# Loading order, wk's transpose and a rewritten order table in a fused attention and FFN kernel

## The chip, the core and the metric

The kernel runs on one core of a Trainium2 chip. Times are device microseconds (us) of one execution; the comparison is between medians of runs of the kernel before and the kernel after. PE is the tensor engine (PEld its weight loads), DVE the vector engine, ACT the scalar engine, POOL GpSimd, SP the engine that here only issues DMAs.

## What is computed

For 2048 tokens of width 640, `g * a + (1 - g) * b`: a gate of its own for each token, a linear attention `a` of 32 heads of 20, and a gated FFN `b` of width 1728.

```python
qkv = x @ wqkv                                        # q, k, v, each [32 heads, 2048, 20]
pq, pk = q @ w_phi, k @ w_phi                         # for each head
phi = lambda p: concat(softmax(p), softmax(-p))       # 40 features for each head
kv, z = phi(pk).T @ v, phi(pk).sum(over tokens)
o = (phi(pq) @ kv) / (phi(pq) @ z + 1e-6)
a = o @ wo
b = (silu(x @ w_gate) * (x @ w_up)) @ w_down
g = sigmoid((x * gate_w).sum(-1))
```

## The kernel before, in words

The tokens are cut into 16 tiles of 128 (`NT`), and for the FFN and the output into four blocks of 512. Everything is bf16 with sums in PSUM. All instructions are written out once, and `_Tracker` puts the semaphore waits in. What the program does is a list of items, `ORDER`, in which each item is a letter, a tile or block, and sometimes a part. An engine's instructions run in the order in which the items stand in this list, so the list is the schedule of all five engines. The items:

- `H` warming matmuls on ones (`NWARM` = 4 each); `G` gate_w's column, put beside wv; `X t` five PE transposes of an x tile (`xpose`).
- `V t` v of a tile and the gate's sum; `U` the first V tiles, their five chunks of wv interleaved, so that the work starts when the first chunk lands.
- `W m` five PE transposes of a row block of wk into `wT` (`wxpose`); `Y` w_phi laid out as blocks `wbd`; `M m` and `R m` premultiply wk and wq with w_phi (`premult`), so that k's and q's projections give pk and pq at once.
- `K t` projects a k tile, takes exp(p) and exp(-p) on ACT into `ekr`, sums (DVE), reciprocals (DVE), and the product with them on POOL. `E t` adds phi(k).T v into PSUM banks 6 and 7, which the item `I` takes out of the ring of pairs of banks and `N` (`kv_finish`) puts back. `Z` broadcasts z by matmul into `zb`.
- `Q t` projects a q tile and takes both exponentials into `eq` (three buffers); `A` sums them (`qz`, DVE); `B` is the DVE product `ez` = eq * zb; `C` gives the denominators on DVE, then the scaled phi(q) `ph` on POOL and its transposing DMA to `phiT` on SP's queue.
- `F b.k` 128 columns of w_gate and w_up for a block: ten matmuls of 512 columns, tanh and a copy on ACT, a product on DVE that reads PSUM, a product on POOL into `hT`. `O b.part` is phi(q) times kv, `D b.u` one output tile: 19 pairs of matmuls with `wd`, `wog`, an ACT scaling by the gate, the store.
- `L` issues the loads of all FFN weights and of wo; `T` copies the last 64 columns of the two FFN weights side by side; `J` gives the gates.

Loads stand ahead of the list. SP's queue has x tile 0, three chunks of wv, then transposing DMAs of x tiles 2 and 3, five plain loads of wk, and transposing DMAs of x, wq and x. ACT's has gate_w, x tile 1, two chunks of wv and w_phi. `ring` gives out four pairs of PSUM banks in turn (three while the kv sums stand), and an item that gets a pair waits until its last user has been read out. `slab` is one stretch of SBUF with different tiles in different stages.

The lines that the prediction names are helpers': L284 is every matmul, L296 PE's transposes, L302 ACT, L308 copies, L312 products of two tensors (`tt`), L316 and L323 DVE, L337 and L338 transposing and plain DMAs.

Of the kernel before, what the change touches and what calls it, by code (L numbers as in the profile page):

```python
# [14 lines left out]
NCH = 11  # L15
NPE = 2
NV = 6
# [11 lines left out]


ORDER = """
H2 H0 H3 H1 L H5 H4 G X0 X1 U V2 W0 W1 Y V3 W2 W3 I W4 M2 M1 M0 M4 M3 K0 K1 K2 V4 K3 V5 R0 E0 V6
E1 K4 V7 K5 R1 E2 K6 E3 V8 K7 V9 E4 V10 E5 K8 K9 E6 V11 E7 R3 K10 K11 R2 E8 F0.0 E9 V12 K12 K13
F0.1 E10 V13 K14 E11 R4 F0.2 K15 V14 Q0 A0 V15 E12 F0.3 E13 E14 E15 N F1.0 Q1 A1 Z B0 F0.4 J Q2
C0 F1.1 B1 F1.2 C1 F1.3 F0.5 A2 Q3 F0.6 F0.7 A3 B2 F0.8 F1.4 F0.9 B3 Q4 F0.10 T C2 F1.5 F1.6 C3
F1.7 F0.11 A4 F1.8 Q5 Q6 F0.12 F0.13 F1.9 F1.10 A5 O0.0 B4 O0.1 O0.2 F1.11 B5 F1.12 C4 A6 Q7 B6
D0.0 C5 A7 Q8 C6 D0.1 D0.2 B7 Q9 C7 A8 F1.13 D0.3 Q10 A9 B8 F2.0 C8 A10 O1.0 O1.1 B9 O1.2 F2.1
F2.2 C9 Q11 B10 C10 D1.0 F2.3 Q12 A11 B11 D1.1 D1.2 Q13 F2.4 F2.5 A12 A13 F2.6 F2.7 F2.8 C11 F2.9
D1.3 B12 C12 F2.10 F3.0 F2.11 B13 Q14 A14 F3.1 Q15 A15 F3.2 F2.12 B14 F3.3 O2.0 C13 F2.13 F3.4
F3.5 B15 F3.6 O2.1 O2.2 F3.7 F3.8 C14 D2.0 F3.9 D2.1 C15 F3.10 F3.11 F3.12 O3.0 O3.1 O3.2 F3.13  # L40
D2.2 D2.3 D3.0 D3.1 D3.2 D3.3
"""
# [145 lines left out]
def _build(nc, A_x, A_wqkv, A_w_phi, A_wo, B_x, B_w_gate, B_w_up, B_w_down, gate_w, out):  # L188
# [30 lines left out]
    omg = sb("omg", [P, NT], F32)  # L219
    ksum = sb("ksum", [P, 2, 64], F32)  # L220
    krec = sb("krec", [P, 2, 66], F32)
    v1r = sb("v1r", [P, NV, 33 * 21], BF16)
# [9 lines left out]

    hbase = nc.lookup_mloc(hT).addr
    ekr = nc.alloc_sbuf_tensor_at("ekr", [P, 4, FK], BF16, offset=hbase + 14 * 512 * 2)
    tr.reg(ekr, "sbuf", hbase + 14 * 512 * 2)

# [14 lines left out]
    oT = at("oT", [P, 2, 5, 512], BF16, 2 * 4 * NCH * P * 2)  # L251
    xs = at("xs", [P, 6, D], BF16, 0)
    wkn = at("wkn", [P, 5, D], BF16, 7680)
    wTq = at("wTq", [P, 5, 5, P], BF16, 14080)
    wT = at("wT", [P, 5, 5, P], BF16, 20480)
    wbd = at("wbd", [P, 5, 160], BF16, 26880)
    wph = at("wph", [P, 5, DH], BF16, 28480)
    bmask = at("bmask", [P, 5, 8], BF16, 28736)
    gwr = at("gwr", [P, P], BF16, 28864)

# [67 lines left out]
    def memset(e, a, v):  # L328
        eo = tr.eng[e]
        return run(e, lambda: eo.memset(a, v), [], [a])  # L330
# [16 lines left out]


    x2 = A_x[0]
    out2 = out[0]  # L350

    def load_x(t, e="sp"):
        if t < NPE:
            dma(e, xs[:, t, :], x2[t * P:(t + 1) * P, :])
        else:
            dma("sp", xT[:, t, :, :], x2[t * P:(t + 1) * P, :], transpose=True)

    def load_rows(e, dst, c, c0):
        dma(e, dst, A_wqkv[c * P:(c + 1) * P, c0:c0 + D])

    dma("act", gwr[0:5, :], bass.AP(gate_w.tensor, gate_w.offset, [[P, 5], [1, P]]))
    load_x(0)
    load_x(1, "act")
    for c in range(5):
        load_rows("act" if c % 2 else "sp", wvg[:, c, 0:D], c, 2 * D)
    load_x(2)
    dma("act", wph[:, :, :], A_w_phi.rearrange("h e f -> (h e) f").rearrange("(c p) f -> p c f", p=P))
    load_x(3)
    for c in range(5):
        load_rows("sp", wkn[:, c, :], c, D)  # L370
    for t in range(4, 7):
        load_x(t)
    for m in range(5):
        dma("sp", wTq[:, m, :, :], A_wqkv[m * P:(m + 1) * P, 0:D], transpose=True)
    for t in range(7, NT):
        load_x(t)
    memset("pool", ident[:, :], 0.0)
# [6 lines left out]
    for c in range(5):  # L384
        b0 = P * c - DH * H0[c]
        select(bmask[:, c, :], [[-DH, 8]], ALU.is_ge, 0.0, b0, 1)
        select(bmask[:, c, :], [[DH, 8]], ALU.is_gt, 0.0, DH - b0, -1)
    v1v = v1r[:, :, :].rearrange("p b (h d) -> p b h d", d=DH + 1)
    memset("dve", ones[:, :], 1.0)
    memset("dve", v1v[:, :, H, :], 0.0)  # L390
    memset("dve", v1v[:, :, :, DH:DH + 1], 1.0)
    memset("dve", ekr[:, :, 1280:FK], 0.0)
# [9 lines left out]

    def load_ffn_weights():
        for c0, c1 in ((0, 512), (512, 1152), (1152, F_FFN)):
            dma("sp", wg[:, :, c0:c1], B_w_gate[:, c0:c1].rearrange("(c p) j -> p c j", p=P))
            dma("sp", wu[:, :, c0:c1], B_w_up[:, c0:c1].rearrange("(c p) j -> p c j", p=P))
        dma("sp", wd[:, 0:13, :], B_w_down[0:13 * P, :].rearrange("(c p) j -> p c j", p=P))
        dma("sp", wd[0:64, 13, :], B_w_down[13 * P:F_FFN, :])
        wo_a = A_wo[0:600, :].rearrange("(m s r) j -> s r m j", s=2, r=60)
        dma("sp", wog[0:60, :, :], wo_a[0])  # L410
        dma("sp", wog[64:124, :, :], wo_a[1])
        dma("sp", wd[64:104, 13, :], A_wo[600:640, :])
# [35 lines left out]
    def v_out(t, pr):  # L448
        i = halves(pr).rearrange("p b (h d) -> p b h d", d=DH)
        o = v1v[:, t % NV, 0:H, 0:DH].rearrange("p (b h) d -> p b h d", b=2)  # L450
        copy("act", o, i)
        copy("act", svec[:, t:t + 1], bank(2 * pr + 1, 320, 321))
# [5 lines left out]

    def vfirst():

        prs = [next_pair(), next_pair()]
        pairs = [v_pairs(t, prs[t]) for t in range(2)]
        for c in range(5):
            for t in range(2):
                mm(pairs[t][2 * c:2 * c + 2])
        for t in range(2):
            v_out(t, prs[t])

# [17 lines left out]
    def ktile(t):  # L486
        pr = tok_proj(t, 1, t == 0)
        b = t % 4
        s = t % 2
        e = ekr[:, b, 0:1280]  # L490
        head_exps(pr, e)
        reduce(ksum[:, s, :], e.rearrange("p (g d) -> p g d", d=DH))
        recip(krec[:, s, 0:64], ksum[:, s, :])
        ev = e.rearrange("p (g d) -> p g d", d=DH)
        tt("pool", ev, ev, krec[:, s, 0:64].unsqueeze(2).to_broadcast([P, 64, DH]), ALU.mult)

    KV0 = 6

    def kvtile(t):
        b = t % 4  # L500
        pairs = []
        for j in range(NCH):
            bk, jj = (KV0, j) if j < 8 else (KV0 + 1, j - 8)
            o = bank(bk, 63 * jj, 63 * jj + 63)
            pairs.append((o, ekr[:, b, 120 * j:120 * j + P], v1r[:, t % NV, 63 * j:63 * j + 63],
                          t == 0 and jj == 0, t == NT - 1, True))
        mm(pairs)

    def wxpose(m):
        pr = next_pair()  # L510
        o = bankbf(2 * pr, 640)
        transposes([(o[:, c * P:(c + 1) * P], wkn[:, m, c * P:(c + 1) * P]) for c in range(5)])
        copy("dve", wT[:, m, :, :].rearrange("p c k -> p (c k)"), o)

# [72 lines left out]
    def qscale(t):  # L587
# [13 lines left out]
            in1=qd[:, s, :].unsqueeze(2).to_broadcast([P, 32, 2]), op0=ALU.mult, op1=ALU.mult),  # L601
            [qz[:, b, :], qd[:, s, :], g2[:, t:t + 1]], [qc[:, s, 0:64]])
        f = ph[:, b, :].rearrange("p (j c) -> p j c", c=P)[:, :, 0:120]
        tt("pool", f.rearrange("p j (g d) -> p j g d", d=DH),
# [52 lines left out]
    out_evs = []  # L657

    def ditem(bt, u):
        buf = bt % 2  # L660
# [10 lines left out]
        if t < NT - 1:  # L671
# [3 lines left out]
            return  # L675
        mm(half[0])
        actop(o[:, 0:320], bank(2 * pr, 0, 320), ACTF.Copy, omg[:, t:t + 1])
        out_evs.append(dma("sp", out2[t * P:(t + 1) * P, 0:320], o[:, 0:320]))
        mm(half[1])
        actop(o[:, 320:D], bank(2 * pr + 1, 0, 320), ACTF.Copy, omg[:, t:t + 1])  # L680
        out_evs.append(dma("act", out2[t * P:(t + 1) * P, 320:D], o[:, 320:D]))


# [3 lines left out]
    def kv_end():  # L687
        kv_finish()
        ring["n"] = 4

    ops = {
        "H": lambda i: warm(), "X": xpose, "G": gcol, "U": vfirst, "V": vtile, "W": wxpose,
        "M": lambda m: premult(1, m), "R": lambda m: premult(0, m),
        "K": ktile, "E": kvtile, "L": load_ffn_weights, "T": tail_weights, "J": gates,
        "Y": w_blocks, "I": kv_begin, "N": kv_end, "Z": z_broadcast,
        "Q": qtile, "A": qsum, "B": qden, "C": qscale,
        "F": fitem, "O": oitem, "D": ditem,
    }
    for w in ORDER.split():
        ops[w[0]](*[int(a) for a in w[1:].split(".") if a])  # L700
# [4 lines left out]
def bass_gated_mix__linear_kernel_hedgehog__swiglu_ffn__prompt_kernel(  # L705
    nc: bass.Bass,
    A_x: bass.AP,
    A_wqkv: bass.AP,
    A_w_phi: bass.AP,
    A_wo: bass.AP,  # L710
    B_x: bass.AP,
    B_w_gate: bass.AP,
    B_w_up: bass.AP,
    B_w_down: bass.AP,
    gate_w: bass.AP,
    out: bass.AP,
):
    with nc.Block() as block:
        @block.gpsimd
        def _(g):  # L720
            _build(nc, A_x, A_wqkv, A_w_phi, A_wo, B_x, B_w_gate, B_w_up, B_w_down, gate_w, out)

# [27 lines left out]
```

The softmax here doesn't subtract the row's maximum and nothing guards it: scores larger than these inputs give would overflow.

## Time and profile before

| what | value |
|---|---|
| median of 9 runs | 294.62 us (294.2 to 297.71) |
| the profiled execution, its own time | 295.07 us |
| its span, first to last instruction | 293.1 us |
| HBM read and written | 9.45 MB, 2.62 MB |
| transposing DMAs of x, of wq, of ph | 14, 5, 16 |
| mean granted TensorE clock in the record | 1.000 |

The page's busy times tell how full an engine is, not what a change is worth. The chain of waits names who ended last, a timeline gives each group's start, and the distance from one group's start to the next is its cost on that engine, since matmuls overlap and the time shown for one of them is longer than its pace. The clock's record begins only after the first microseconds; there the pace of equal matmuls tells the clock.

### The profile page before, as it was taken

How to read it: one execution, taken by the hardware profiler on the slowest of the kernel's cores; microseconds unless marked ns; L12 is line 12 of the kernel's file. 1: busy time of each engine (PE TensorE's matmuls, PEld its weight loads, DVE VectorE, ACT ScalarE, POOL GpSimd, SP SyncE). 2: the span in 40 equal slices, each digit the busy share in tenths (PEclk: the TensorE clock that was granted, in tenths of full speed). 3: DMA queues.
4: the chain of work that ended last, by engine and by line, in shares of the span. 5: the costliest groups of instructions: out<-in, count | busy, mean ns of one | idle time of the engine just before them, and what ended most of it. 6: DMA issues, size and time to landing. Idle time of an engine off the chain costs nothing.

```text
span 293.1 us, 4885 instructions
## 1 busy us (share of the span) xinstructions
PE 287.7 (98%) x1971; PEld 174.8 (60%) x1971; DVE 168.4 (57%) x248; ACT 148.6 (51%) x252; POOL 157.5 (54%) x118
## 2 busy tenths in 40 slices
PE   8999999999999999999999999999999999999996
PEld 6767776666445545447765567646454466457774
DVE  2566858656898779269973994077657654110000
ACT  1476767674756555682344833352476642472112
POOL 8719769785258758745451565046755844530000
PEclk9999999999999999999999999999999999999999
DMA  8878799520003102200542025100320203300101
GB/s 211 199 113 111 181 360 361 137 56 0 2 4 70 25 2 49 49 2 9 108 111 61 11 42 121 46 0 0 74 49 0 49 2 72 75 0 25 45 22 46
DMA packets 47048, 21.26 MB, mean 73 GB/s; under 512 B 37106, under 2 KB 47026, under 8 KB 47026
## 3 DMA queue, kind: packets, MB, share of 16 engines
q1 hardware_dynamic: 45784, 20.36, 29.4%
q10 hardware_dynamic: 1242, 0.60, 0.7%
q8 instruction: 15, 0.25, 0.4%
q14 instruction: 7, 0.06, 0.1%
HBM read 9.45 MB, written 2.62 MB: 41 GB/s over the span
## 4 chain that ended last, share of the span: by engine, by line
PE 92%; DVE 3%; DMA 2%; ACT 1%; POOL 1%; issue 0%
PE ps L284 91%; DMA phiT<-ph 2%; POOL ph L312 1%; DVE dz L312 1%; PE ps L296 1%; DVE qw L323 0%; DVE hT L316 0%; ACT hT L302 0%; DVE kvsb L312 0%; DVE wqk L308 0%; ACT v1r L302 0%; ACT osb L302 0%; DVE xT L308 0%; DVE wT L308 0%; DVE qd L326 0%
## 5 line engine op out<-in xcount | busy, mean ns | idle before, releaser
L312 POOL TENSOR_TENSOR hT<-hT,us 128x512 bf16<-128x512 bf16 (+1 forms) x56 | 68.4, 1232 | 60.6 <-DVE hT L316 56.7
L316 DVE SCALAR_TENSOR_TENSOR hT<-hT,ps 128x512 bf16<-128x512 bf16 (+1 forms) x56 | 37.8, 680 | 61.3 <-ACT hT L302 54.2
L284 PE MATMUL ps<-xT,wg 128*128 128x512 bf16 x260 | 64.6, 379 | 0.2
L284 PE MATMUL ps<-xT,wu 128*128 128x512 bf16 x260 | 64.6, 379 | 0.0
L284 PE MATMUL ps<-wd,hT 128*128 128x320 bf16 x448 | 63.7, 299 | 0.0
L302 ACT ACTIVATE hT<-ps 128x512 bf16<-128x512 f32 (+2 forms) x60 | 35.8, 596 | 50.8 <-PE ps L284 50.4
L312 POOL TENSOR_TENSOR ph<-eq,qc 128x1320 bf16<-128x1320 bf16 x16 | 39.8, 2488 | 28.3 <-DVE qc L599 28.3
L284 PEld LDWEIGHTS ps<-wd,hT 128*128 128x128 bf16 x448 | 43.9, 98 | 17.8
L284 PE MATMUL ps<-wqk,xT 128*128 128x320 bf16 x320 | 47.8, 299 | 0.0
L312 POOL TENSOR_TENSOR ekr<-ekr,krec 128x1280 bf16<-128x1280 bf16 x16 | 37.4, 2359 | 16.0 <-DVE krec L326 16.0
L284 PEld LDWEIGHTS ps<-xT,wu 128*128 128x128 bf16 x260 | 25.5, 98 | 30.7
L284 PEld LDWEIGHTS ps<-xT,wg 128*128 128x128 bf16 x260 | 24.9, 98 | 28.5 <-ACT us L302 1.1
L302 ACT ACTIVATE osb<-ps,omg 128x640 bf16<-128x640 f32 (+1 forms) x17 | 12.9, 761 | 55.3 <-PE ps L284 55.3
L284 PEld LDWEIGHTS ps<-wqk,xT 128*128 128x128 bf16 x320 | 30.9, 98 | 13.8 <-ACT wqk L302 0.2
L302 ACT ACTIVATE us<-ps 128x512 bf16<-128x512 f32 (+1 forms) x56 | 33.2, 592 | 0.1
L323 DVE TENSOR_REDUCE ksum<-ekr 128x64 f32<-128x1280 bf16 x16 | 23.4, 1464 | 16.9 <-ACT ekr L302 16.9
L302 ACT ACTIVATE eq<-ps 128x640 bf16<-128x640 f32 x32 | 22.4, 703 | 14.6 <-POOL ph L312 9.6
L302 ACT ACTIVATE ekr<-ps 128x640 bf16<-128x640 f32 x32 | 22.1, 703 | 7.1 <-PE ps L284 6.6
L323 DVE TENSOR_REDUCE qz<-eq 128x64 f32<-128x1280 bf16 x16 | 23.6, 1480 | 3.3 <-ACT eq L302 3.3
L284 PE MATMUL ps<-wvg,xT 128*128 128x320 bf16 (+1 forms) x160 | 25.1, 306 | 0.1
L284 PE MATMUL ps<-wog,oT 128*128 128x320 bf16 x160 | 24.5, 299 | 0.0
L323 DVE TENSOR_REDUCE qw<-ez 128x64 f32<-128x1280 bf16 x16 | 23.6, 1478 | 0.1
(71 smaller groups left out, 191.4 us busy)
## 6 DMA issues: line engine op xcount, KB each, us to landing
out_dram<-osb SPq DMA_DIRECT2D x15, 160.0 KB, 1.9
wd<-in_B_w_down_dram SPq DMA_DIRECT2D x1, 2080.0 KB, 17.1
wkn<-in_A_wqkv_dram SPq DMA_DIRECT2D x5, 160.0 KB, 3.2
wg<-in_B_w_gate_dram SPq DMA_DIRECT2D x1, 800.0 KB, 9.0
wu<-in_B_w_up_dram SPq DMA_DIRECT2D x1, 800.0 KB, 10.6
wog<-in_A_wo_dram SPq DMA_DIRECT2D x2, 375.0 KB, 6.8
wg<-in_B_w_gate_dram SPq DMA_DIRECT2D x1, 720.0 KB, 11.5
wu<-in_B_w_up_dram SPq DMA_DIRECT2D x1, 720.0 KB, 11.7
```

The source lines that it names most:

```text
L284: last = pe.matmul(o, lhsT=l, rhs=r, start=st, stop=sp_, skip_group_check=sk)
L296: last = pe.transpose(o, i, ident[0:k, 0:k])
L302: return run("act", lambda: act.activation(o, i, func, scale=scale), rd, [o])
L312: return run(e, lambda: eo.tensor_tensor(o, a, b, op), [a, b], [o])
L316: return run("dve", lambda: dve.scalar_tensor_tensor(out=o, in0=a, scalar=s, in1=b, op0=op0, op1=op1), rd, [o])
L323: return run("dve", lambda: dve.tensor_reduce(o, i, AX.X, ALU.add), [i], [o])
```

## The change

- x tiles 0 to 3 come by plain loads on SP's and ACT's queues and are transposed on PE; the other 12 by transposing DMA. All loads of x, wv, wk and wq stand in a list `LOADS`, with the first 384 columns of the FFN weights ahead of the transposing DMAs.
- wk is loaded by transposing DMA into `wT`; item `W` is gone.
- v of all 16 tiles is kept: six tiles in `v1r`, ten in `v1x`, which lies where `wd` is loaded later. `L` now holds only w_down and wo and stands after the last E.
- `ekr` moves from the place of `hT`'s second buffer to `slab`, so that F items of block 1 may stand before the last E. `ksum` and `krec` get four buffers.
- `K`'s sums and product become items `S` and `P`, `C`'s product and DMA item `c`. `U` becomes one item for a tile and a chunk.
- The last output tile is made in three pieces (320, 224, 96 columns), the last scaled on DVE.
- The program is no longer wrapped in a block of its own.
- The order table is new.

```diff
-NPE = 2
+NPE = 4
...
+LOADS = """
+x0 w0 x1 w1 w2 x2 w3 w4 x3 f0 h k0 k1 t4 k2 k3 k4 t5 t6 t7 t8 t9 t10 t11 t12 t13 t14 t15 q0 q1 q2 q3
+q4 f1 f2
+"""
 ORDER = """
...
+H2 H4 H0 H1 H3 X0 G X1 U0.0 U0.1 U1.0 U0.2 U1.1 X2 U1.2 U0.3 U1.3 U0.4 U2.0 U1.4 U2.1 X3 U2.2 U2.3
+U2.4 V3 Y F0.1 M0 F0.2 M1 M2 F0.0 M3 M4 V4 K0 S0 K1 V7 K2 I P0 V6 S1 P1 K3 S2 E0 K4 S3 V5 P2 P3
+V14 V15 R1 S4 E1 K5 V9 E2 E3 K6 P4 R4 S5 E4 K7 K8 P5 S6 P6 V12 V8 S7 E5 P7 K9 S8 S9 E6 P8 R0 F1.2
+E7 K10 V13 E8 P9 S10 P10 K12 F1.1 R2 S12 P12 V10 E9 K11 K13 E10 S11 V11 P11 J F0.11 T R3 S13 P13
+F0.4 K14 E11 S14 K15 S15 Q1 P15 F1.13 F0.5 F1.8 F0.13 F1.3 E12 P14 F1.11 A1 E13 F0.10 Q2 E14 E15 N
+Q0 F0.12 A0 Z L B0 F1.9 C0 c0 B2 F1.7 F1.12 Q3 A2 C2 c2 B1 F0.8 F0.6 A3 F0.9 C1 c1 Q5 B3 F1.5 C3
+c3 B5 Q4 F0.7 F1.6 F0.3 A5 A4 F1.4 Q6 B4 F1.0 F1.10 C4 C5 c4 A6 O0.2 O0.0 B6 c5 O0.1 C6 Q7 Q8 D0.0
...
+A15 F2.10 c14 F3.6 F3.9 F2.4 C13 F2.6 F2.7 B15 F3.8 F3.12 c13 D2.0 C15 F3.10 D2.1 c15 F3.4 D2.2
+O3.2 O3.1 O3.0 D2.3 D3.2 D3.1 D3.0 D3.3
 """
...
+    v1x = nc.alloc_sbuf_tensor_at("v1x", [P, NT - NV, 33 * 21], BF16, offset=wdbase)
...
+    ekr = at("ekr", [P, 4, FK], BF16, 0)
+    xs = at("xs", [P, NPE, D], BF16, 10752)
...
+    XQ = ["sp", "act", "act", "sp"]
+    WQ = ["sp", "sp", "act", "sp", "act"]
...
+    def load_ffn(c0, c1):
+        dma("sp", wg[:, :, c0:c1], B_w_gate[:, c0:c1].rearrange("(c p) j -> p c j", p=P))
+        dma("sp" if c0 else "act", wu[:, :, c0:c1], B_w_up[:, c0:c1].rearrange("(c p) j -> p c j", p=P))
...
+    def load_wt(which, m):
+        dst = wT if which else wTq
+        dma("sp", dst[:, m, :, :], A_wqkv[m * P:(m + 1) * P, D * which:D * which + D], transpose=True)
+
+    FCUT = [0, 384, 1024, F_FFN]
...
+    def knorm(t):
+        s = t % 4
+        e = ekr[:, t % 4, 0:1280]
         reduce(ksum[:, s, :], e.rearrange("p (g d) -> p g d", d=DH))
         recip(krec[:, s, 0:64], ksum[:, s, :])
...
+    def kmul(t, e="pool"):
...
-    def wxpose(m):
...
+        for b, c0, c1, e in ((2 * pr, 0, 320, "sp"), (2 * pr + 1, 320, 544, "sp"), (bank_free(pr), 544, D, "act")):
+            mm([(bank(b, 0, c1 - c0), l, r[:, c0:c1], i == 0, i == n - 1, False) for i, (l, r) in enumerate(ls)])
+            if e == "act":
+                run("dve", lambda: dve.tensor_scalar(o[:, c0:c1], bank(b, 0, c1 - c0), omg[:, t:t + 1], None,
...
-    with nc.Block() as block:
...
+    _build(nc, A_x, A_wqkv, A_w_phi, A_wo, B_x, B_w_gate, B_w_up, B_w_down, gate_w, out)
```

## The prediction

> **What bounds the kernel now.** The page comes first: which engine is full, and who stands on the chain that ended last.
>
> ```profile
> PE 287.7 (98%) x1971; PEld 174.8 (60%) x1971; DVE 168.4 (57%) x248; ACT 148.6 (51%) x252; POOL 157.5 (54%) x118
> ...
> PE 92%; DVE 3%; DMA 2%; ACT 1%; POOL 1%; issue 0%
> ```
>
> TensorE is on the chain for 92% of the span, no other engine is busy for more than 57%. So time can only be won where TensorE works at half pace, does work that another unit could do, or waits. Next, the waits of PE:
>
> ```profile
> PE ps L284 <- DVE ones L330: 1.1, 1, 1.1
> PE ps L284 <- DVE kvsb L312: 0.6, 1, 0.6
> PE ps L284 <- DMA phiT<-ph: 0.3, 1, 0.3
> ```
>
> Apart from the start there are two: z's broadcast waits for kv_finish, the last attention products wait for a transposed phi. The rest is at the beginning; the timeline of PE there, with the first K tile as its last line:
>
> ```profile
> 5.21 5.13 PE L284 MATMUL ps<-wvg,xT 128*128 128x320 bf16 x30
> ...
> 10.18 0.72 PE L296 MATMUL ps<-ident,wkn 128*128 128x128 bf16 x10
> ...
> 10.74 1.54 PE L284 MATMUL ps<-wvg,xT 128*128 128x320 bf16 x10
> ...
> 12.12 0.72 PE L296 MATMUL ps<-ident,wkn 128*128 128x128 bf16 x10
> ...
> 13.16 0.44 PE L296 MATMUL ps<-ident,wkn 128*128 128x128 bf16 x5 [0.33 <-ACT svec L302]
> 13.54 1.13 PE L284 MATMUL ps<-wbd,wT 128*128 128x140 bf16 x18
> ...
> 14.95 0.80 PE L284 MATMUL ps<-wbd,wT 128*128 128x140 bf16 x12 [0.27 <-DVE wqk L308]
> 15.68 1.58 PE L284 MATMUL ps<-wqk,xT 128*128 128x320 bf16 x10
> ```
>
> From start to start: V 5.21 to 10.18 and 10.74 to 12.12, wk's 25 transposes 0.56 + 1.04 + 0.38 = 1.98 us, the premultiplications 2.14 us. From 15.68 on PE runs without a gap but for the waits named. Steady paces there, start to start: K or Q tile 1.36, V tile 1.38, F item 2.16, output tile 5.17.
>
> **The change, part by part.**
>
> *wk by DMA.* 25 transposes leave PE: -1.98 us. Their five DVE copies go too (487 ns each, not on the path). x tiles 2 and 3 move from DMA to PE: 10 transposes at the 0.056 us pace of wk's: +0.56. The premultiplications (30 matmuls, 1.6 us at their own pace of 0.053) also stood 0.54 us, most of it for a copy of wqk before 14.95; now F items of 2.16 us stand between them and cover that copy: -0.54. First V: X0 can start when the 20 (not 24) warming matmuls end, about 3.3 instead of 3.91, but x1 (landed 4.39) and wv's second chunk (landed 5.38) still come when they came, so -0.1. Sum for the beginning -2.06; I take **-2.0** (-2.8 if the slow pace that PE's first V matmuls show for 1.6 us is not met at all, since it costs half of that; -1.6 if it lasts 0.8 longer).
>
> What covers the moved loads, with each queue:
>
> ```profile
> 2.68 2.64 SPq L337 DMA_TRANSPOSE xT<-in_A_x_dram x2
> ...
> 7.88 3.85 SPq L337 DMA_TRANSPOSE xT<-in_A_x_dram x3
> 11.76 7.32 SPq L337 DMA_TRANSPOSE wTq<-in_A_wqkv_dram x5
> 19.12 12.91 SPq L337 DMA_TRANSPOSE xT<-in_A_x_dram x9
> ```
>
> A transposing DMA holds SP 1.28 us (with pauses 1.4), a plain one 0.46. SP now issues five plain loads and wg's first columns (0.81 to 3.7), then k0 k1 t4 k2 k3 k4: k4 leaves at 10.3 and has landed by 15.0 (3.0 to 4.7 us to landing). ACT issues seven plain loads until 4.2 and its table load (1.28), done before its first eviction (8.73 before). PE reaches F0.1 at 12.1 (V3's end), then F0.1 M0 F0.2 M1 M2 F0.0 M3 M4 with M4 at 19.9: wk's DMAs hide behind 6.5 us of F work; without those items M4 would stand for 2.5 us. F0.1 itself needs 2.46 MB landed by 12.1; the loads of before moved 2.34 MB by 10 us (234 GB/s in that stretch), so 10.5 to 11.5: hidden with 0.6 us or more. V14 and V15 are used early, at 32.8 and 34.2; t15 is the 17th transpose, issued by 3.7 + 16 x 1.4 = 26.1 and landed by 31. R1 at 35.6 needs q1, landed by 34. f1 and f2 leave SP at 33 to 35 as the FFN loads did (32.1), landed by 48.7 before; first use at 65 (F0.11). All at nothing; each first use that is late costs its own lateness.
>
> The table's name is not quite what it does: V10 to V13 still stand behind K8. It costs nothing, since PE does the same tiles.
>
> *wd behind the last E.* v1x lies on wd, so wd's load waits on SP for E15 (PE at 90), and the second half of wog for the first (8.9 us on SP before): SP is held from 90 to about 100. Behind it stands phiT's first DMA, wanted at 103. Nothing; wd is first read at 132.
>
> *The new order around z.* Before, z's first product took the PSUM pair of the kv sums and waited for kvsb (0.72 us over the pace of a matmul). Counting pairs in the new table, N resets the ring so that z's first pair is free and only its second is the kv pair; Q0 and F0.12 (3.5 us) stand over the 3.70 us from zt to the last kvsb. **-0.65** (-0.72 to -0.3, should the DVE be 0.35 late).
>
> *Attention's first tiles.* Here the new order takes its risk: 14 F items stand before N instead of four, so the DVE work of Q0 to Q8 meets less matmul work. I add up the DVE in its order from B0, start to start (F 0.60, A 1.40, C 2.84). For B the rows give two prices:
>
> ```profile
> L312 DVE TENSOR_TENSOR ez<-eq,zb x16: 806/819/2668, 77.7 to 231.3; 128x1280 bf16<-128x1280 bf16 x16
> ```
>
> The slow ones ran against POOL's ph (one starts at 84.53, ph at 84.10 to 86.52). The new table puts B directly behind C, so that ez starts before POOL hears of qc: I take 0.8. zb is out at 96.2 (after z, behind F0.12 on ACT). Then four B, seven F, two A, four C: 3.2 + 4.2 + 2.8 + 11.4 = 21.6, C3 done at 117.8; ph 2.4 and the phiT DMA (3.5 to 5.1) give 123.8 to 125.4. O0 stands on PE at 127.7: 2.2 us or more to spare. PSUM: F1.5 at 109.9 needs F0.8's pair, freed at 108.0. Nothing.
>
> *The end of the attention.* O3 waited 0.51 over the pace for phiT. Now c15 follows F3.10's product on POOL (249.6 to 252.1), DMA until 257.3, O3 at 259.7: **-0.4** (-0.5 to -0.2). O2's three parts stand together, one change of tile shape less (0.1 in, 0.1 out): **-0.2**.
>
> *The last tile.* Three pieces instead of two: the last is 96 columns on the DVE. By DVE rows (128x16 0.167, 128x640 out of PSUM 0.818) 0.25 against ACT's 0.53; 19 more matmuls cost 0.1; a hand-over from DVE to ACT's queue 0.05: **-0.15** (0 to -0.3). Without the block its closing barrier (292.78 to 293.07 in the trace) goes: **-0.25** (0 to -0.3).
>
> *New small waits.* More separate groups at the start and more changes between projections and F items: a group that waits costs about 0.045 (the gap at 16.37); five or six of them **+0.25** (0 to 0.8).
>
> Sum: -2.0 - 0.65 - 0.4 - 0.2 - 0.15 - 0.25 + 0.25 = -3.4. The profiled execution took 295.07 us (span 293.07), 0.45 above the median of 294.62. From 295.07 that is 291.67, on the median's scale **291.2 us**. With every term at its good end it is -4.8, at its bad end -1.4 (O2 -0.1): this case's own range is 289.8 to 293.2.
>
> **Two rules.** PE's pace shows its clock: V's first matmuls come every 0.267 us until 6.8, then every 0.138. The Trainium skill, "TensorE: Matmul & The Clock Gate", says in Part 1 that the clock opens after a busy window of some 3.4 us, and in Part 4 that transposes don't count as busy in the same way. That speaks against fewer warming matmuls and more transposes; by it the switch could come one window later, which would be 3.4 x (1 - 0.138/0.267) = 1.6 us as an estimate and 292.8 in sum. Its window is not visible here, and the changed start keeps V's first matmuls where they were, so I book the row.
>
> "DMA: Bandwidth & Descriptors", under Issuing engines are not separate DMA queues, says that a second queue saves only issue time. The row: seven loads of 160 KB landed from 3.17 to 6.39, one each 0.54, slower than the 0.46 of an issue. By rule and row the two queues bring nothing themselves, and nothing is booked for them.
>
> **The rivals.**
>
> *The beginning is given back.* Clock or data come late. A slow stretch from the first V twice as long (1.6 us more) costs 0.8 us; F0.1's columns at 12.9 instead of 11.5 another 0.8. For it: DMA is full from 4 to 8 us. Against: nine loads at 0.54 end at 7.5, before their use. 292.0 to 293.2.
>
> *Slower: the DVE becomes the bound at O0.* If ez loses the port to POOL each time, four B cost 1.86 more each, 7.4 us; less the 2.2 to spare, O0 waits 5.2: 296.4. It decides from 3.4 us of waiting on (two to three lost), and is slower by 0.5% from 4.9. For it: the mean ez took 1288 ns, and 46 us of DVE work (N 3.7, 14 F, 6 A, 7 B, 7 C) lie against 42 of PE between N and D0.0. Against: the slow ez of the trace began after ph, never before. With one or two lost: 291.2 to 292.7; with three 294.5.
>
> *Nothing moves.* The steady part was full before; if the early F work only shifts stalls, 293.2 to 296.
>
> **How the numbers follow.** The forecast has 0.64, the beginning given back 0.14 (nearly all still faster), nothing moved 0.11, the slower one 0.11. A measurement of this kernel can tell about 0.5%, 1.5 us: faster is below 293.15, slower above 296.1. So faster 0.77, same 0.12, slower 0.11. The range takes the forecast, the given-back start and half of the cases that move nothing: 289.8 to 294.4.
>
> **What would show it.** The changed trace should have the first K tile at 21.5 with three F items and V4 before it (13.7 without them), no PE wait above 0.2 at z and O3, ez at a mean near 0.9 us, O0 unbroken near 127. A PE wait for DMA before 36 us, or for phiT or an F product between 105 and 130, would prove the sum wrong.

## The result, and the profile after

The changed kernel takes 291.94 us (median of 21 runs, 290.29 to 293.89); the kernel before took 294.58 us in the 63 runs beside them (293.95 to 297.77). The ratio is 0.9897, 95% interval 0.988 to 0.9915. The profiled execution of the changed kernel took 290.8 us, its span is 289.3; that of before had 295.07 and 293.1. So the profiled pair differs by 4.3 us and the medians by 2.6. Most of what follows is about that 1.6.

First PE's busy time and the chain that ended last, from the page of the changed kernel:

```profile
PE 285.6 (99%) x1971; PEld 174.8 (60%) x1971; DVE 167.0 (58%) x248; ACT 147.8 (51%) x252; POOL 157.8 (55%) x118
...
PE 98%; DMA 1%; ACTq 0%; issue 0%; DVE 0%
```

PE's part of the chain grew from 92% to 98%; DVE's 3% and the transposing DMA's 2% are gone. All of PE's waits (us in total, times, longest):

```profile
PE ps L294 <- DVE ones L340: 1.1, 1, 1.1
PE ps L306 <- DMA xs<-in_A_x_dram: 0.5, 1, 0.5
```

The waits for kvsb and phiT that before showed are no longer there; the new one is X1 waiting for x tile 1. PE's timeline at the beginning (start, us, engine and line), with the first F item, the premultiplications, V4 and the first K tile:

```profile
4.56 0.71 PE L306 MATMUL ps<-ident,xs 128*128 128x128 bf16 x5 [0.47 <-DMA xs<-in_A_x_dram]
5.06 2.52 PE L294 MATMUL ps<-wvg,xT 128*128 128x320 bf16 x10
...
10.12 2.37 PE L294 MATMUL ps<-wvg,xT 128*128 128x320 bf16 x16
12.33 1.24 PE L294 MATMUL ps<-xT,wg 128*128 128x512 bf16 x5
...
19.75 0.79 PE L294 MATMUL ps<-wbd,wT 128*128 128x140 bf16 x12
20.38 1.54 PE L294 MATMUL ps<-wvg,xT 128*128 128x320 bf16 x10
21.75 2.47 PE L294 MATMUL ps<-wqk,xT 128*128 128x320 bf16 x17
```

First F at 12.33 and first K at 21.75, where 12.1 and 21.5 were forecast. Less V4 (20.38 to 21.75) and three F items of 2.16, K stands at 13.90, against 15.68 before: the beginning gained 1.8 us here. The end, from the timeline of all engines:

```profile
287.00 0.38 PE L294 MATMUL ps<-wog,oT 128*128 128x96 bf16 x5
287.42 0.32 DVE L697 TENSOR_SCALAR osb<-ps,omg 128x96 bf16<-128x96 f32 x1 [31.26 <-PE ps L294]
287.76 0.37 ACTq L348 DMA_DIRECT2D out_dram<-osb  x1
```

From the start of the last matmul (287.17) to the end of the span (289.27) it is 2.10 us; before it was 2.83 (290.24 to 293.07), with these last lines:

```profile
290.57 0.53 ACT L302 ACTIVATE osb<-ps,omg 128x320 bf16<-128x320 f32 x1 [2.06 <-PE ps L284]
291.13 0.36 ACTq L338 DMA_DIRECT2D out_dram<-osb  x1
```

### The profile page after: what moved, and what is told of

Read it like the earlier page. It is cut to its first block, busy times and chain, and to the rows that moved or that the text cites. A ratio compares the mean times of both kernels' runs of the same rounds, so it can differ in the third digit from the quotient of the medians.

```text
span 289.3 us, 4874 instructions
## 1 busy us (share of the span) xinstructions
PE 285.6 (99%) x1971; PEld 174.8 (60%) x1971; DVE 167.0 (58%) x248; ACT 147.8 (51%) x252; POOL 157.8 (55%) x118
## 4 chain that ended last, share of the span: by engine, by line
PE 98%; DMA 1%; ACTq 0%; issue 0%; DVE 0%
PE ps L294 97%; DMA xs<-in_A_x_dram 1%; PE ps L306 0%; ACTq L348 0%; DVE osb L697 0%
## 5 line engine op out<-in xcount | busy, mean ns | idle before, releaser
L322 POOL TENSOR_TENSOR hT<-hT,us 128x512 bf16<-128x512 bf16 (+1 forms) x56 | 66.1, 1191 | 58.9 <-DVE hT L326 58.8
L294 PE MATMUL ps<-wd,hT 128*128 128x320 bf16 (+2 forms) x462 | 63.9, 295 | 0.0
L322 POOL TENSOR_TENSOR ph<-eq,qc 128x1320 bf16<-128x1320 bf16 x16 | 42.3, 2645 | 25.2 <-DVE qc L610 23.1
L312 ACT ACTIVATE osb<-ps,omg 128x640 bf16<-128x640 f32 (+2 forms) x17 | 12.9, 757 | 48.2 <-PE ps L294 48.2
L294 PE MATMUL ps<-wog,oT 128*128 128x320 bf16 (+2 forms) x165 | 24.7, 295 | 0.0
```

Source lines behind the costliest of these rows:

```text
L294: last = pe.matmul(o, lhsT=l, rhs=r, start=st, stop=sp_, skip_group_check=sk)
L312: return run("act", lambda: act.activation(o, i, func, scale=scale), rd, [o])
L322: return run(e, lambda: eo.tensor_tensor(o, a, b, op), [a, b], [o])
```

## The experiments

The theory was the sum of the prediction: early F items hide wk's DMAs, z and O3 lose their waits, the end gets shorter. Its rivals were a beginning given back to data or clock, and a DVE that loses the port to POOL. The first question was why the median gained less than the profile.

**The changed kernel again, three times.** No edit. 

> The changed kernel unchanged, as the base for the others and to see what its runs scatter over (290.3 to 293.9 us, where the kernel before has most runs within 294.0 to 295.1). If the scatter is in the span, spans go from 289.0 to 291.4 and the trace's start (arrival of x1 and of the first chunks of wv, the moment when PE's pace doubles) or a late DMA differs from the first trace. If it lies outside of the span, the time less the span is 1.2 in some runs and 2.4 in others. Median 291.9 (291.6 to 292.3).

 

> The changed kernel unchanged once more, as the base of this call: median 291.8 (291.3 to 292.3). By e1 and e2 its PE waits at the start and at R1 follow the landings of wv, x, wu and wq and differ from execution to execution; this trace should show another set of them (0.5 to 2.5 us in sum before 37 us) and the same rest.

 

> The changed kernel unchanged, as the base of this call: 291.8 to 292.7 us, time less span between 1.2 and 2.9 us in two groups.

Measured 291.78 us (6 runs), 292.63 (9) and 292.44 (12), ratios to before 0.9904, 0.9936 and 0.9914. The third one's trace has this beginning:

```profile
7.29 1.27 PE L294 MATMUL ps<-wvg,xT 128*128 128x320 bf16 x8 [1.61 <-DMA wvg<-in_A_wqkv_dram]
...
13.59 1.24 PE L294 MATMUL ps<-xT,wg 128*128 128x512 bf16 x5
```

wv's second chunk landed at 7.24 us here, at 5.27 in the first trace. Eight traces share the items of this beginning (the first, these three, and those of the old end, the later ez, z's pairs and the block alone, below). Their first F item starts at 12.20, 12.32, 12.33, 12.79, 12.94, 13.07, 13.59 and 14.07 us. From there to the first K it is 9.42 and 9.43 in two of them and 9.63 to 9.80 in six: M0 starts 0.2 to 0.4 late. From the first K to the last matmul the first trace needs 265.42, and so do, within 0.06, those of the loads, z, block and x1 variants; the three repetitions need 265.7 to 265.9, and all of that difference stands at one place: R1 starts 0.27 to 0.48 late, behind the landing of wTq. So up to 1.9 us differ ahead of the first F item, and up to 0.4 and 0.5 in the two stretches behind it.

Pooled, the 49 executions without an edit have a median span of 290.5 (289.0 to 292.6): the profile's 289.3 was one of the short ones. The kernel before has a median span of 292.6 to 292.7, and its profiled 293.1 was one of the longer. So the spans of the profiled pair differ by 3.8 us and the median spans by 2.1, and that is where the 1.6 us between the profiled pair and the medians lie. The time outside of the span is nearly the same in the mean: 1.86 us before, 1.81 in these 49.

**F items behind V15, without and with warming.** The F items that stand between the premultiplications are moved behind V15; then twelve warming items (48 matmuls on ones) are put in their place.

```diff
-U2.4 V3 Y F0.1 M0 F0.2 M1 M2 F0.0 M3 M4 V4 K0 ... V14 V15 R1
+U2.4 V3 Y M0 M1 M2 M3 M4 V4 K0 ... V14 V15 F0.1 F0.2 F0.0 R1            (first kernel)
+U2.4 V3 Y H6 ... H17 M0 M1 M2 M3 M4 V4 K0 ... V14 V15 F0.1 F0.2 F0.0 R1 (second kernel)
```

> The changed kernel with F0.1, F0.2 and F0.0 moved from between the premultiplications of wk to behind V15: PE has the same work. My theory: the F items are the cover of wk's transposing DMAs. In the trace wk's last row block landed at 17.96, so M4 waits for it from 13.9 on and the first K tile starts at 19.7 where it would start at 15.3 without a wait: 4.0 to 4.5 us slower than e1, 296.2, no better than the kernel before. Rival: the gain is the PE work that was removed, and the order at the start doesn't matter: within 0.5 of e1.

 

> e3 (the three early F items behind V15) with 12 warming items, 48 matmuls on ones, put into the place where PE waited 2.65 us there. They compute nothing that is used. My theory: in e3 the wait itself cost 3.5 us in three places, and another 1.7 us because PE ran at half pace from 17.3 to 20.8 us; with PE kept busy the clock stays and e8 is 1.2 to 1.9 us faster than e3: 295.8 to 296.4. Rival: the half pace has nothing to do with the wait: within 0.5 of e3.

Without warming 297.66 us, 1.0097 of before (1.0059 to 1.0136), 5.9 over the changed kernel measured beside it. PE in its trace, from x tile 3's transposes to the first K tile, with the waits in brackets:

```profile
10.39 0.44 PE L306 MATMUL ps<-ident,xs 128*128 128x128 bf16 x5
...
15.68 1.68 PE L294 MATMUL ps<-wbd,wT 128*128 128x140 bf16 x24 [2.65 <-POOL wbd L322]
17.97 0.78 PE L294 MATMUL ps<-wbd,wT 128*128 128x140 bf16 x6 [0.61 <-DMA wT<-in_A_wqkv_dram]
...
21.00 2.88 PE L294 MATMUL ps<-wqk,xT 128*128 128x320 bf16 x20
```

The long one is for w_phi's blocks, since w_phi landed at 14.02; wk's own wait is 0.6. And a stretch of the same trace, busy us (instructions) of PE, PEld, DVE, ACT and POOL, then the granted clock (0.51), the share of the DMA engines and GB/s:

```profile
17.30:20.80 3.50, 2.89 (x16) 1.90 (x16) 1.27 (x2) 0.70 (x1) 0.00 (x0) 0.51 0.93 120
```

The clock fell to half from 17.34 to 20.76 us, after PE had stood from 13.03 to 15.68. With warming it stays at 1.00 from 14 us on:

```profile
17.33 0.49 PE L294 MATMUL ps<-wbd,wT 128*128 128x140 bf16 x6 [0.55 <-DMA wT<-in_A_wqkv_dram]
...
19.03 1.25 PE L294 MATMUL ps<-wqk,xT 128*128 128x320 bf16 x8
```

M4 and V4 in front of the first K take 1.70 us there and 3.03 at the half clock, so the clock costs 1.3 of the 1.97 by which K0 is earlier; the other 0.6 are an earlier landing of wk's last block. The time is 295.76, 1.9 less, of which the median spans show 1.4 (295.85 and 294.5). The rest lies outside of the span. Five of the six executions without warming have a granted clock under 1.00; the sixth has 1.00, and its 295.76 us is the median with warming.

K0 at 21.00 is 5.7 us behind where the changed kernel would have it without the F items (21.75 less three times 2.16 = 15.27). But this execution was 0.5 late already ahead of the place, with x tile 3's transposes at 10.39 instead of 9.85. So the F items cover 5.2 us, about twice the 2.5 of the prediction: it knew of M4's wait, but not of w_phi's, and priced no clock.

**wk's DMA alone.** The kernel before, with only wk's plain loads and transposes replaced.

```diff
-    for c in range(5):
-        load_rows("sp", wkn[:, c, :], c, D)
+    for m in range(5):
+        dma("sp", wT[:, m, :, :], A_wqkv[m * P:(m + 1) * P, D:2 * D], transpose=True)
```

All `W` items leave the order, and the ring is set forward by their five pairs. 

> The kernel before with one part of the change alone: wk by transposing DMA in place of five plain loads, PE's transposes of wk left out, PSUM pairs afterwards as before. PE has 25 transposes less (1.98 us of PE time). My theory: without F items to cover them the DMAs are waited for. They leave SP at 5.4 to 10.6, the last lands at 14.5 to 15.5, the first K tile starts at 15.5 to 16.1 against 15.68: the time is the same as before, -0.2 to +0.5. Rival: PE work alone counts: 1.5 to 2 us faster, 292.7.

294.67 us (12 runs), ratio 1.0001 (0.998 to 1.0021): nothing. K0 starts at 15.55 instead of 15.68, although 1.98 us of transposes are gone. Two of PE's waits:

```profile
PE ps L283 <- POOL wbd L311: 1.7, 1, 1.7
PE ps L283 <- DMA wT<-in_A_wqkv_dram: 0.6, 1, 0.6
```

The transposes had been covering w_phi's blocks and wk's landing. Here w_phi itself had landed at 7.37, but POOL was filling buffers until 11.5 and made its share of the blocks only then, until 12.72. In addition the clock is at half from 14.76 to 18.18 in this execution; that is so in three of the twelve (granted clock 0.994), and the nine others have a median of 294.21, no more than 0.2 below the 294.41 of the kernel before beside them. So it is not the clock that ate the 1.98. Taking work off PE is worth nothing at this place unless other work goes there.

**Loads by order of use.** Only `LOADS` is changed: w_phi ahead of the first FFN columns, x tiles 7, 6, 5, 14, 15 and wq's block 1 in the order in which PE takes them.

```diff
-x0 w0 x1 w1 w2 x2 w3 w4 x3 f0 h k0 k1 t4 k2 k3 k4 t5 t6 t7 t8 t9 t10 ... t15 q0 q1 q2 q3
+x0 w0 x1 w1 w2 x2 w3 w4 x3 h f0 k0 k1 t4 k2 k3 k4 t7 t6 t5 t14 t15 q1 t9 q4 t8 t12 q0 t10 ...
```

> The changed kernel with nothing but the list of loads reordered: w_phi ahead of the first FFN columns, and the transposing DMAs in the order in which PE uses them (x tiles 7 6 5 14 15, then wq's second block, 9, wq's fifth, ...). My theory: the forecast's missing 0.7 us are waits for landings: wq's second block (0.3 and 0.6 us in e1 and e2) and w_phi before the first premultiplication (0.2) go, 0.4 to 0.8 us faster than e5, with no PE wait for a DMA between 14 and 70 us. Rival: the scatter lies in the first 12 us alone (x and wv), then the same median as e5.

292.63 us, just as the changed kernel beside it; the means differ by 0.04, with an interval of -0.7 to +0.8. R1's wait is gone and PE waits for no DMA after 14 us, so those waits were real, and their 0.3 to 0.5 us are too small to show in runs that scatter so. Its trace has the first F item only at 14.17 (x1 landed at 5.09, and PE's pace doubled only at 10.1). Most of the scatter is not in the later loads.

**x tile 1 first.**

```diff
-    dma("act", gwr[0:5, :], bass.AP(gate_w.tensor, gate_w.offset, [[P, 5], [1, P]]))
     def load_x(t):
         dma(XQ[t], xs[:, t, :], x2[t * P:(t + 1) * P, :])
+        if t == 1:
+            dma("act", gwr[0:5, :], bass.AP(gate_w.tensor, gate_w.offset, [[P, 5], [1, P]]))
...
-H2 H4 H0 H1 H3 X0 G X1 U0.0
+H2 H4 H0 H1 H3 X0 H6 X1 G U0.0
```

> x tile 1 goes ahead of gate_w's small load on ACT's queue, and one warming item stands between X0 and X1, G after X1. Theory A (the first 12 us are bound by landings, and the idle spot of 0.5 us before X1 lets the clock open late): X1 no longer waits, V's first matmuls begin 0.3 to 0.5 us earlier, the clock opens earlier in most executions, median 0.3 to 0.8 us below the changed kernel's of the same call. Rival B (w1 at 5.3, x3 at 7.6 and the data of the first FFN columns bind anyway): V3 ends where it did, at 12.2 to 12.4 us, and the median is within 0.3 us.

291.87 us (6 runs, 290.65 to 292.23), ratio 0.9891 (0.9853 to 0.9928). Its mean is 0.8 under that of the changed kernel beside it (interval 0.2 to 1.45), but not for theory A's reason:

```profile
6.01 2.17 PE L294 MATMUL ps<-wvg,xT 128*128 128x320 bf16 x10 [0.56 <-DVE wvg L318]
...
12.93 1.24 PE L294 MATMUL ps<-xT,wg 128*128 128x512 bf16 x5
```

x1 landed at 3.81 instead of 4.51 (and x0 at 3.62 instead of 3.15), but V starts 0.95 us later, since it waits for gate_w's column, which now comes last. So theory A had no fair trial here. The first F stands within the scatter of the others, and so do the spans (median 290.6). Half of the difference lies outside of the span (1.23 to 1.29 in all six runs, 1.2 to 2.6 in the base). For the spans alone the mean gain is 0.4 and not clear of the scatter (interval -0.3 to 1.1). So no cause is shown.

**ez behind POOL's ph.** `B2`, `B1`, `B3` and `B5` each go one F item later, so that ez comes after POOL has begun with ph.

```diff
-C0 c0 B2 F1.7 ... C2 c2 B1 F0.8 ... C1 c1 Q5 B3 F1.5 C3 c3 B5 Q4 F0.7
+C0 c0 F1.7 B2 ... C2 c2 F0.8 B1 ... C1 c1 Q5 F1.5 B3 C3 c3 Q4 F0.7 B5
```

> The changed kernel with four items moved by one F item, B2, B1, B3 and B5 behind the next F item, so that ez starts after POOL's ph and not before it: the same work. My theory (the rival of the forecast that ends slower): ez then takes 2 to 2.7 us instead of 0.82, C3 ends 4 to 5.5 us later on DVE, phi of tile 3 lands at 130.5 to 132 instead of 126.6, and the first product with it, at 127.8, waits 3 to 4 us: 294.5 to 296, more if the wait closes PE's clock for a while. Rival: DVE is no bound here, ez gets slower and the time stays within 0.5 of e5.

296.19 us, 1.0047 of before (1.0027 to 1.0068), 3.6 over the changed kernel beside it. The ez group (least, median and most ns) of the changed kernel, and then of this one:

```profile
L322 DVE TENSOR_TENSOR ez<-eq,zb x16: 816/820/1927, 96.5 to 237.1; 128x1280 bf16<-128x1280 bf16 x16
```

```profile
L322 DVE TENSOR_TENSOR ez<-eq,zb x16: 814/860/2670, 96.6 to 241.3; 128x1280 bf16<-128x1280 bf16 x16
```

Four are at 2.67 now. ez started at 100.69 and ph at 100.86 in the changed kernel, and took 0.82 and 2.94; here ph starts at 100.95 and ez at 101.39, and they take 2.42 and 2.67. Either way the pair is done 3.1 us after the first start; who starts first only decides who is held. PE pays elsewhere than the rival said:

```profile
PE ps L294 <- DVE hT L326: 3.0, 4, 1.7
```

F and Q items wait for PSUM that has not been read out, four times by the late DVE and once by ACT: 0.66, 0.55, 0.40, 0.64 and 1.83 over the pace, in sum 4.1 us between 112 and 128 us. O0 starts at 132.01 instead of 127.83.

**z's pair.** z takes the pair of the kv sums first, as before the change.

```diff
+        other = next_pair()
         pr = next_pair()
...
-        pr = next_pair()
+        pr = other
```

> z takes the PSUM pair of the kv sums first, as before the change, and the free pair second; nothing else differs. Theory A (the forecast's): the wait at z went away because the free pair comes first; with the kv pair first PE waits 0.65 us again for kvsb. Theory B: Q0 and F0.12 alone cover it, since dz took 1.53 us in the changed kernel against 2.19 before, and the last kvsb copy ended at 93.49, ahead of z's start at 93.68: a wait of 0 to 0.1 us. Up to 0.35 us would mean that both have a share.

291.23 us in its one run. z in PE's timeline, with the F item's last five matmuls ahead of it:

```profile
93.30 1.24 PE L294 MATMUL ps<-xT,wu 128*128 128x512 bf16 x5
94.38 0.72 PE L294 MATMUL ps<-dz,ones 120*128 120x480 bf16 x3
```

No wait at all, and from first K to last matmul the same 265.42 us as in the changed kernel. So the pair's order is worth nothing here; Q0 and F0.12 alone cover the DVE's chain. But they do so only because the chain got shorter: dz took 1.53 us in the changed kernel and here, and 2.19 before. Here the last kvsb copy ended at 94.19, 0.19 ahead of z, so with the old dz z would have waited some 0.5 (an estimate from these times), and the pair's order would have counted. Before, dz (71.97 to 74.17) met a product `hT` on POOL (71.62 to 72.78); in the changed kernel POOL's last one ended at 90.86 and dz began at 90.88.

**The old end, and the block alone.** The first kernel has the block and the last tile in two halves again, the second the block only.

```diff
-    _build(nc, A_x, A_wqkv, A_w_phi, A_wo, B_x, B_w_gate, B_w_up, B_w_down, gate_w, out)
+    with nc.Block() as block:
+        @block.gpsimd
+        def _(g):
+            _build(nc, A_x, A_wqkv, A_w_phi, A_wo, B_x, B_w_gate, B_w_up, B_w_down, gate_w, out)
```

> The changed kernel with the block around the program and the last output tile in two halves, as before. My theory: the end of the span gets longer by the block's barrier (0.25 to 0.3) and by the tile (0.15): from the last matmul's start to the end of the span 2.5 to 2.6 us against 2.1, median 0.4 above e1. Rival: without the block the program's end is only waited for elsewhere, so the time doesn't move, or it scatters less than e1.

 

> The changed kernel inside a block again, its last tile in three pieces. Theory A (the forecast's: the block's closing barrier costs 0.25 us and nothing more): median 0.2 to 0.3 us above the changed kernel's of the same call. Theory B (without the block the time outside of the span scatters, 1.2 to 2.9 us, where with a block it is 1.7 to 1.8): time less span is 1.7 to 1.8 again in each run, and the spread of the times gets smaller. With both, the median may stand anywhere from -0.1 to +0.4.

Both: 292.34 us, 0.6 over the changed kernel beside it; the means differ by 0.5, with an interval of -0.3 to +1.25. The block alone: 293.0, 0.6 over the changed kernel beside it, but the means differ by 0.35 with an interval of -0.24 to +0.99. So the times settle neither theory. The traces say more: from the start of the last matmul to the span's end 2.83 us with both, 2.36 with the block alone, 2.10 with neither (2.10 to 2.20 in the ten traces with this end). The barrier is 0.26; the three pieces are 0.47, less 0.145 that PE needs for more matmuls (5.18 against 5.035 for the tile).

Time less span was 1.7 to 1.8 in all six runs with both, but 1.74 to 2.88 with the block alone and 1.2 to 2.9 in the pooled runs without it (26 of 49 from 1.2 to 1.52, the rest from 1.83 on). So theory B, that the block makes this time steady, is wrong. The least of it does go with the block: none of the 102 executions with a block whose span is on record has less than 1.67, while 60 of 94 without it have 1.2 to 1.55. What scatters it upward from there stays open.

The block alone had the latest first F item of the eight, and mostly for another reason than late data (0.28 us are a wait for wv):

```profile
8.08 0.74 PE L306 MATMUL ps<-ident,xs 128*128 128x128 bf16 x5
8.62 2.91 PE L294 MATMUL ps<-wvg,xT 128*128 128x320 bf16 x14
...
14.07 1.24 PE L294 MATMUL ps<-xT,wg 128*128 128x512 bf16 x5
```

Five transposes take 0.74 us at 8.08, as at the very start, and 0.44 from 7.42 on in the first trace: this execution still ran at half pace, until about 10.3, where the first trace did until about 7.0. So late data and a late clock each happen, and in these two traces they cost 1.3 and 1.7 us.

## Why the prediction was right, and where its sizes were not

The direction and the range held, 291.94 against 291.2 and within 289.8 to 294.4, and so did the mechanism of the largest term: F items as cover for wk's DMAs. The step on z held in half. That the sum came so near is in part luck: it was made from one profiled execution, and where it has 3.4 us, the profiled pair shows 4.3 and the medians 2.6. One of its signs of being wrong did come: PE waits for DMA before 36 us. The 0.5 for x1 was in the sum, as a landing that does not move; R1's 0.3 to 0.6 and the waits for wv of up to 1.6 in other executions were not. Step by step:

| step | forecast | shown |
|---|---|---|
| beginning | -2.0 | -1.8 in the profiled pair (K at 13.90 for 15.68); in eight traces the first F item stands up to 1.7 later, 0.5 in the middle of them |
| z | -0.65 | wait gone; not by the pair, but by cover and a shorter dz |
| O3, O2 | -0.4, -0.2 | O3's wait gone (0.1 over the pace), O2 in one stretch; neither was tried alone |
| last tile | -0.15 | -0.33 (0.47 less 0.145) |
| block | -0.25 | -0.26 in the span; outside of it up to 0.45 in some executions, which was not forecast |
| small waits | +0.25 | none in the profiled execution; in the repetitions 0.2 to 0.4 up to the first K and 0.3 to 0.5 at R1 |

*The beginning* is the term that was mis-sized. The forecast had V's first matmuls at the place and pace of one trace, and put the given-back start aside as a rival of 0.14. The median execution stands between the two: its span is 1.2 us over the profiled one, of which the traces place some 0.5 ahead of the first F item and the rest in the small waits behind it. Two things were missed. "Hidden" was argued from landings of one execution, while wv's second chunk lands anywhere from 4.9 to 7.24. And the clock's opening varies: by PE's pace and the clock's record it opens between 4.6 and 7.1 us in seven of the eight traces and at 10.3 in the eighth. The forecast weighed the Trainium skill's rule here ("TensorE: Matmul & The Clock Gate", Part 1) and booked the row. The rule's later opening is real in the block-alone trace: 3.3 us behind the first trace's, near the one window of the forecast's estimate, and the first F item is 1.7 later (14.07 against 12.33) where the estimate had 1.6. In the first trace the row was right.

*The loads' times* were forecast too early. SP's queue in the changed kernel:

```profile
3.64 3.20 SPq L347 DMA_TRANSPOSE wT<-in_A_wqkv_dram x2
6.88 3.42 SPq L347 DMA_TRANSPOSE xT<-in_A_x_dram x1
10.35 3.92 SPq L347 DMA_TRANSPOSE wT<-in_A_wqkv_dram x3
```

Three of these should have taken 3.9 us, as the last line shows, but the first three took 6.6: behind the plain loads one took 1.8 and one 3.4. k4 landed at 17.96, not at 15.0, still ahead of M3 and M4 at 19.75; q1 landed at 35.72, not by 34, and R1 pays 0.3 to 0.6 for it in some executions. With the 1.8 us to spare there, most of the price stayed nothing.

*z*: the step named two reasons, the pair and the cover. Only the cover counts, and it had 0.19 to spare only because dz takes 0.66 less, which the step did not see.

*Attention's first tiles*: the DVE sum was 2.3 us short (C3 done at 120.1, not 117.8; phiT landed at 126.63, not 123.8 to 125.4), and the slack at O0 was 1.2, not 2.2. The term that was short is C, priced at 2.84 from start to start: C0 took 2.85, C2, C1 and C3 3.20, 3.70 and 3.81. In each of the three a small sum or product of 0.22 us took 0.57 to 1.08, and ended 0.1 us after a product `hT` on POOL that was running:

```profile
117.91 1.15 POOL L322 TENSOR_TENSOR hT<-hT,us 128x512 bf16<-128x512 bf16 x1
...
118.06 1.08 DVE L605 TENSOR_TENSOR qm<-qw,qz 128x64 f32<-128x64 f32 x1
```

So it was not ez alone that met POOL; the forecast priced the meeting for ez and not for C. The mean ez was 0.995 us where 0.9 was forecast. The order of B directly behind C did what the step said. The slower rival was a real price, shown by moving four B, with the same size of loss (O0 4.2 later where 5.2 was worked out), but it comes in by the PSUM of F and Q items and not by phiT at O0.

*The end* gained more than booked. Only the shorter eviction had been counted (0.53 to 0.32 us, 0.25 forecast); the last matmul's start to the eviction also went from 0.34 to 0.24, and the store from issue to landing from 1.62 to 1.46.

*wk by DMA* behaves as the cover argument said, only more so: alone it gives nothing, and without cover it costs 5.2 us up to the first K.

## What to carry to other kernels

Work taken from the bounding engine is gained only where something else stands ready for the hole: ask what else the removed work was hiding (here w_phi's blocks as well as wk), and price the clock with the wait. A stage that starts from cold data has a spread, not a place; take its landings from several executions, or forecast its gain from the later ones. Where two engines share a port, the order in which their instructions start is part of the schedule.

## What was not expected of the hardware

- The granted clock fell to half for one stretch of 3.41 us although PE had been busy for about half of the stretch of that length before it: 1.75 us idle from 13.93 to 17.34 in the F-later kernel, 2.1 idle in the wk-alone one. The half-paced stretch begins 1.7 to 1.9 us after the long wait has ended.
- The profile's clock column says 1.00 from 6 to 10 us in the block-alone trace, while transposes and matmuls there go at half pace. In these first microseconds only the pace tells the clock.
- One transposing DMA held SP's queue for 3.42 us where most later ones hold it for 1.28, while the plain loads were still landing.
- ez and ph don't share the port's time: the one that starts first runs at its own 0.82 or 2.42 us, and the other ends at the same 3.1 us after the first start. The Trainium skill, "SBUF — State Buffer", in SBUF: two separate sides, calls this an exclusive lock held for a whole instruction; the numbers agree to 0.15 us. dz beside `hT`, and the small sums of C beside it, look the same.
